# Softmax of the first four attention tiles on ScalarE, set by set, and an ordering-only dependency in the schedule planner

## The chip, the cores and the metric

One core of one Trainium2 chip. The metric is the device time in microseconds of one execution. Three runs of the kernel before lie between 1133.39 and 1134.48 us, with a median of 1134.45 us.

## The reference

Three stages run one after the other on 3072 tokens.

1. Chunked attention: batch 4, 8 heads, 768 positions, head size 64. Chunks of 32 queries see 8 memory keys and a window of 16 positions on the left, their own 32, and 8 on the right: 64 keys at most (fewer at the two ends of the sequence). Scores are `scale * q·k` with scale 1/8, then a softmax (`exp(s - max)`, divided by `sum + 1e-9`), then the product with the values.
2. A gated feed-forward layer: `(sigmoid(x @ w_gate) * (x @ w_val)) @ w_out`, with 512 features and 1536 hidden ones.
3. A second feed-forward layer with a rational function in place of the gate: `h = x @ w_in`, `P(h) / Q(|h|)`, `@ w_out`, with 2048 hidden features.

All in float32.

## The kernel before, in words

The 3072 tokens are 24 attention tiles of 128. A tile is 128 query rows by 8 sets (heads) of 64 keys, so its scores are 128x512. The weights come in as a packed form of 8 bytes an element: per unit of 128x512, two ScalarE operations (`conv_scale`: tile names `st` and `stp`) and one VectorE operation (`conv_bits`, into `wfgv` or `wfo`) make float32 of them. Each matmul operand is then split into a high part (ScalarE copy, `split_hi`) and a low part (VectorE subtraction, `split_lo`), both in the tile `wp`; three matmuls stand for one float32 product. A hidden block f of the first layer takes three units: 0 and 1 are the two halves of the contraction for gate and value together, 2 is the output weight.

The first four tiles (t = 0 to 3) make up the start of the kernel, together with the conversion of the weights of blocks 0, 1 and 2. TensorE's order there is written out by hand: scores (`sp`) of tile 0, 1, 2, 3, transposes (`tp`) of tiles 0 and 1, the value product (`xp`) of tile 0, transposes of tiles 2 and 3, value products of tiles 1, 2 and 3, with matmuls on a tile of ones (`idle`) in between, and then the first products of block 0 (`h`). PSUM has four banks for all of these (pool `ps`), given out in turn: `sp` takes two, `tp` one, `xp` two, a group of `h` one.

Softmax of one of these tiles before the change:

- `attn_max` (L584): VectorE takes the maximum over the keys (one pass over 512 columns where the scores have been copied to SBUF because of the mask, which is tile 0; else two passes over 256 in PSUM), then subtracts it (as many passes), into the SBUF tile `s`.
- `attn_exp`: one ScalarE activation of 128x512.
- `attn_sum`: VectorE sums 512 columns into 8 sums (`r`), adds 1e-9, takes the reciprocal. `attn_mul` multiplies.

Tiles 4 to 7 use the same functions later on, between the blocks of the first layer. Tiles 8 to 23 use other functions (`pair_max` and so on).

The order of work on each engine other than TensorE isn't written by hand. A class `Recorder` keeps each operation as a task with an estimated duration and a latest start (`late`), and `plan()` runs a list schedule over them: each engine takes, of the tasks that are ready in the model, the one with the earliest `late`. The instructions are emitted in that order. Loads (SyncE's DMA queue) are ordered in the same way. A tile's memory is a `Cell`; the first task that touches it is `c.first`, and every other task that touches the cell depends on it in `access` (L275), even where it works on other bytes of it. Two loads of different units into one tile are such a case: the weights of blocks 1 and 2 are loaded by `load_w1` into four tiles named `stp`, two units to a tile, so that units 0 and 1 of a block lie in the same tile.

Of the kernel before, what the change touches and what calls it, by code (L numbers as in the profile page):

```python
# [11 lines left out]
F32 = mybir.dt.float32  # L12
# [4 lines left out]
ACTF = mybir.ActivationFunctionType  # L17
ALU = mybir.AluOpType
AX = mybir.AxisListType
PSUM = bass.MemoryType.PSUM  # L20

B, H, S, D = 4, 8, 768, 64
CH, LEFT, RIGHT, NMEM = 32, 16, 8, 8
NT, DM, DFF1, DFF2 = B * S, H * D, 1536, 2048
P = 128
# [6 lines left out]
KEYS = NMEM + LEFT + CH + RIGHT  # L32
OFF1 = WIN - KEYS
NSET = 8
# [19 lines left out]
class Cell:  # L54


    def __init__(self, pool, make, dt, real=None):
        self.pool, self.make, self.dt, self.real = pool, make, dt, real
        self.accesses, self.users, self.first, self.group, self.left = [], set(), None, None, 0
# [115 lines left out]
class Task:  # L175
    def __init__(self, eng):
        self.eng, self.calls, self.deps, self.cells, self.gets = eng, [], set(), set(), []
        self.dur, self.lat, self.bytes, self.start, self.table, self.mark = 0.0, 0.15, 0, None, None, None
        self.window, self.cap, self.soon, self.late, self.fixed = 30.0, None, 0.0, 0.0, False
        self.ordered = True  # L180
# [10 lines left out]
class Recorder:  # L191
# [48 lines left out]
    def call(self, eng, op, args, kw):  # L240
        out = kw.get("out", args[0] if args else None)
        reads = [x for x in (*args[0 if "out" in kw else 1 :], *kw.values()) if isinstance(x, Ref) and x is not out]
        reads = [x for x in reads if x is not kw.get("out")]
        key = {x.cell for x in reads}
        if eng == "tensor" and out.size() > 128:
            key.add(out.cell)
        same = eng == "tensor" and self.open is not None and self.open.key == key
        if same:
            t = self.open
        else:  # L250
            t = Task(eng)
            t.key, t.fixed, t.soon = key, self.fixed, self.ideal
            self.tasks.append(t)
            if eng == "tensor":
                self.open = t
                t.late = t.soon = self.ideal
            if self.noted is not None:
                self.noted.append(t)
        before = t.dur
        self.cost(t, op, args, kw)  # L260
        if eng == "tensor":
            self.ideal += t.dur - before
        t.calls.append((op, args, kw))
        for x, write in [(x, False) for x in reads] + ([(out, True)] if isinstance(out, Ref) else []):
            self.access(t, x, write)
        if eng != "tensor" and self.open in t.deps:
            self.open = None

    def access(self, t, x, write):
        c, box = x.cell, x.box()  # L270
        if c.pool is not None and t not in c.users:
            if c.first is None:
                c.first = t
                t.gets.append(c)
            elif c.first is not t:  # L275
                t.deps.add(c.first)
            c.users.add(t)
            t.cells.add(c)
        keep = []
        for b, u, w in c.accesses:  # L280
            if b[0] < box[1] and box[0] < b[1] and b[2] < box[3] and box[2] < b[3]:
                if u is not t and (write or w):
                    t.deps.add(u)
                inside = box[0] <= b[0] and b[1] <= box[1] and box[2] <= b[2] and b[3] <= box[3]
                if write and inside or u is t and w == write and inside:
                    continue
            keep.append((b, u, w))
        keep.append((box, t, write))
        c.accesses = keep
# [24 lines left out]
    def plan(self):  # L314
        tasks = self.tasks
        for t in tasks:
            t.succ = []
        for t in tasks:
            t.missing, t.soft = len(t.deps), []
            for d in t.deps:  # L320
                d.succ.append(t)
            t.ready = 0.0
# [6 lines left out]
        for t in reversed(tasks):  # L329
            t.succ, t.hard = t.succ + t.soft, t.succ  # L330
            if t.eng == "tensor":
                t.late = min([t.soon] + [u.late - t.lat * (u.eng != "tensor") - t.dur for u in t.succ])
                continue
            lat = t.lat + (4.5 if t.bytes else 0)
            cap = t.cap if t.cap is not None else self.DMA_CAP if t.bytes else self.CAP
            t.late = min([t.soon + cap] + [u.late - lat - t.dur for u in t.succ])
        free = dict(self.sizes)
        cells = {c for t in tasks for c in t.cells}
        for c in cells:
# [14 lines left out]
        ready = {e: [t for t in tasks if t.eng == e and not t.missing] for e in engines}  # L354
        busy, dma, table = dict.fromkeys(engines, 0.0), 0.0, None
        order, ends, half, now, stall, left = [], [], None, 0.0, 0.0, len(tasks)
        events = []
        self.stalls = []
        while left:
# [3 lines left out]
            for e in engines:  # L363
# [10 lines left out]
                for t in pick:  # L374
# [7 lines left out]
                    need, h = {}, half  # L382
                    for c in t.gets:
                        if c.pool == ("t", "half"):
                            if h:
                                h = None
                                continue
                            h = True
# [8 lines left out]
                t = best  # L397
# [29 lines left out]
                for c in t.cells:  # L427
                    c.left -= 1
                    g = c.group
                    g[2] = max(g[2], end)  # L430
                    if c.left == 0:
                        g[1] += 1
                        if g[1] == 2 or g[1] == g[0] and g is not half:
                            heapq.heappush(ends, (g[2], self.real_pool(c.pool)))
                for u in t.hard:
                    u.missing -= 1
                    u.ready = max(u.ready, end if u.eng != e or e != "tensor" else now + t.dur)
                    if not u.missing and u.eng != "tensor":
                        ready[u.eng].append(u)
                    heapq.heappush(events, u.ready)  # L440
# [4 lines left out]
            if not moved:  # L445
# [5 lines left out]
                for e in engines[1:]:  # L451
                    for t in ready[e]:
                        w = t.late + stall - t.window
# [5 lines left out]
                now = max(nxt, now + 1e-6)  # L459
# [15 lines left out]
def fused_kernel(ctx: ExitStack, tc: tile.TileContext, q, k, v, w1, w2, coef, x2d, w2o, wq2, wqa, wqs, out):  # L475


    nc = Recorder(tc.nc)
    x2d, w2o, wq2, wqa, wqs = (cell_ref(None, None, x.shape, F32, x, True) for x in (x2d, w2o, wq2, wqa, wqs))

    def pool(name, bufs, **kw):
        return Pool(ctx.enter_context(tc.tile_pool(name=name, bufs=bufs, **kw)), name, bufs, nc.sizes)
# [6 lines left out]
    spool = pool("s", 4)  # L489
# [28 lines left out]
    qs, ks, vs, s_sb, sc_ps, at_sb = {}, {}, {}, {}, {}, {}  # L518
# [19 lines left out]
    def edge(t):  # L538
        return t % SB in (0, SB - 1)

    def attn_qk(t):
# [28 lines left out]
        else:  # L570
            sc_ps[t] = sps

    def attn_max(t):
        s = s_sb[t]
        m = spool.tile([P, NSET, 1], F32, tag="m", name=f"m{t}")
        if edge(t):
            nc.vector.tensor_reduce(out=m[:, :, 0], in_=s, axis=AX.X, op=ALU.max)
            nc.vector.tensor_tensor(out=s, in0=s, in1=m.to_broadcast([P, NSET, KEYS]), op=ALU.subtract)
            return
        sv = s.rearrange("p (r h) w -> p r h w", h=2)  # L580
        mv = m.rearrange("p (r h) w -> p r h w", h=2)
        sps = sc_ps.pop(t)
        for h in range(2):
            nc.vector.tensor_reduce(out=mv[:, :, h, 0], in_=sps[h], axis=AX.X, op=ALU.max)  # L584
        for h in range(2):
            nc.vector.tensor_tensor(
                out=sv[:, :, h], in0=sps[h], in1=mv[:, :, h].to_broadcast([P, 4, KEYS]), op=ALU.subtract
            )

    def attn_exp(t):  # L590
        s = s_sb[t]
        nc.scalar.activation(out=s, in_=s, func=ACTF.Exp, scale=1.0 / float(D) ** 0.5)

    rs = {}

    def attn_sum(t):
        s = s_sb[t]
        r = rs[t] = spool.tile([P, NSET, 1], F32, tag="r", name=f"r{t}")
        nc.vector.tensor_reduce(out=r[:, :, 0], in_=s, axis=AX.X, op=ALU.add)
        nc.vector.tensor_scalar_add(out=r, in0=r, scalar1=1e-9)  # L600
        nc.vector.reciprocal(out=r, in_=r)

# [582 lines left out]
    def at(si, *call):  # L1185
        plan.setdefault(si, []).append(call)
# [24 lines left out]
    for t in range(4, NPAIR, 2):  # L1211
        s0 = 2 if t == 4 else 5
        for o, u in ((0, t), (1, t + 1)):
            at(s0 + o - 2, load_qk, u)
            at(s0 + o, attn_qk, u)
            at(s0 + o, attn_max, u)
            at(s0 + 3, attn_exp, u)
            at(s0 + o + 3, load_v, u)
            at(s0 + o + 3, attn_sum, u)
            at(s0 + o + 3, attn_mul, u)  # L1220
            at(s0 + o + 4, attn_t, u)
            at(s0 + o + 5, pv, u)
# [89 lines left out]
    with tc.manual_schedule():  # L1312
# [14 lines left out]
        idle_mm(8)  # L1327
        attn_qk(0)
        attn_max(0)
        attn_exp(0)  # L1330
        idle_mm(2)
        attn_qk(1)
        idle_mm(3)
        attn_qk(2)
        attn_sum(0)
        attn_max(1)
        attn_exp(1)
        attn_max(2)
        attn_sum(1)
        idle_mm(12)  # L1340
        attn_qk(3)
# [724 lines left out]
```

## Time and profile before

| | us |
|---|---|
| median of 3 runs | 1134.45 |
| the profiled execution | 1134.46 |
| its span | 1132.6 |
| TensorE busy | 1120.2 (99%) |
| VectorE busy | 872.8 (77%) |
| ScalarE busy | 750.1 (66%) |
| GpSimd busy | 23.1 (2%) |

The span is what the instructions of the one profiled execution cover; its own time is 1.86 us longer. Busy shares are averages over stages that have different limits. The busy time of TensorE counts the matmuls on the tile of ones too.

### The profile page before, as it was taken

To read this page: it belongs to the slowest core of one execution; us is meant where nothing else is said; L and a number is where in the kernel's file an instruction comes from. 1 tells how busy PE (TensorE), PEld (TensorE's weight loads), DVE (VectorE), ACT (ScalarE), POOL (GpSimd) and SP (SyncE) were. 2 spreads that over 40 slices of the span, in tenths; PEclk is the share of its full clock that TensorE was granted. 3 is DMA by queue.
4 is the path that set the end of the run, shared out by engine and by line. 5 is a ranking of instruction groups with operands and counts; after the bars stand their busy time and mean duration, and the time that the engine had idled before them with its cause. 6 is when DMAs were issued, how large, how long until landed. Compare 5 with 4: busy or idle time off the path is not lost.

```text
span 1132.6 us, 20033 instructions
## 1 busy us (share of the span) xinstructions
PE 1120.2 (99%) x7815; PEld 918.5 (81%) x7815; DVE 872.8 (77%) x1184; ACT 750.1 (66%) x1105; POOL 23.1 (2%) x39
## 2 busy tenths in 40 slices
PE   8999999999999999999999999999999999999998
PEld 4787888888888888888888788888888888888887
DVE  5788867774676667565568499999899999789984
ACT  4999556663454466343345599875799974898852
POOL 0000000000000000000000000000000000000000
PEclk8999999999999999999999999999999999999999
DMA  9899699997978799898976576689677788576764
GB/s 371 311 352 360 227 347 363 350 365 259 379 279 324 288 376 387 310 373 291 322 259 246 191 230 220 208 246 342 203 229 225 223 288 307 167 242 219 230 207 143
DMA packets 100318, 318.78 MB, mean 281 GB/s; under 512 B 10752, under 2 KB 11008, under 8 KB 100224
## 3 DMA queue, kind: packets, MB, share of 16 engines
q1 hardware_dynamic: 96192, 303.51, 74.3%
q0 software_dynamic: 3456, 12.58, 6.0%
q8 instruction: 62, 1.02, 0.4%
q10 hardware_dynamic: 576, 1.41, 0.3%
q14 instruction: 32, 0.26, 0.1%
HBM read 240.91 MB, written 63.96 MB: 269 GB/s over the span
## 4 chain that ended last, share of the span: by engine, by line
PE 96%; ACT 1%; DMA 1%; DVE 1%; issue 0%; DVEq 0%
PE acc L471 40%; PE p L471 20%; PE q_X L471 12%; PE h L471 10%; PE q_Z L471 6%; PE q_Y L471 3%; PE xp L471 2%; PE sp L471 1%; PE tp L471 1%; PE idle L471 1%; DMA st<-w_in 0%; DMA k<-k_in 0%; ACT L471 0%; ACT stp L471 0%; DVE s L471 0%
## 5 line engine op out<-in xcount | busy, mean ns | idle before, releaser
L471 PE MATMUL acc<-w2o,G 128*128 128x512 f32 x1152 | 268.4, 389 | 0.0
L471 PEld LDWEIGHTS acc<-w2o,G 128*128 128x128 f32 x1152 | 216.2, 188 | 44.9
L471 PE MATMUL acc<-g,wp 128*128 128x512 f32 x720 | 177.0, 393 | 0.0
L471 PEld LDWEIGHTS acc<-g,wp 128*128 128x128 f32 x720 | 133.3, 188 | 28.3 <-issue 0.2
L471 PE MATMUL q_X<-x,wi 128*128 128x512 f32 x576 | 146.5, 390 | 1.4 <-ACT hb L471 1.4
L471 PE MATMUL h<-x,wp 128*128 128x512 f32 x576 | 138.1, 392 | 1.7 <-ACT sg L471 0.9
L471 PE MATMUL p<-b,wpq_s 128*128 128x512 f32 x576 | 138.4, 389 | 0.0
L471 PEld LDWEIGHTS q_X<-x,wi 128*128 128x128 f32 x576 | 107.9, 188 | 24.7 <-ACT hb L471 2.5
L471 PEld LDWEIGHTS h<-x,wp 128*128 128x128 f32 x576 | 107.2, 188 | 25.0 <-ACT wp L471 1.1
L471 PEld LDWEIGHTS p<-b,wpq_s 128*128 128x128 f32 x576 | 108.1, 188 | 22.5
L471 ACT ACTIVATE st<-st 128x512 f32<-128x512 f32 (+1 forms) x124 | 76.7, 666 | 0.0
L471 PE MATMUL p<-x,wpq_a 128*128 128x512 f32 x288 | 73.2, 389 | 0.0
L471 PE MATMUL q_Z<-x,wi 128*128 128x512 f32 x288 | 73.1, 389 | 0.0
L471 ACT ACTIVATE u<-q,qc 128x1024 f32<-128x1024 f32 x48 | 54.9, 1147 | 14.4 <-DMA q<-u 13.2
L471 PEld LDWEIGHTS p<-x,wpq_a 128*128 128x128 f32 x288 | 54.0, 188 | 11.3
L471 PEld LDWEIGHTS q_Z<-x,wi 128*128 128x128 f32 x288 | 54.1, 188 | 11.2
L471 DVE SCALAR_TENSOR_TENSOR t<-t,cf,u 128x1024 f32<-128x1024 f32 x48 | 61.2, 1278 | 0.0
L471 DVE SCALAR_TENSOR_TENSOR q<-q,u 128x1024 f32<-128x1024 f32 x48 | 58.3, 1219 | 2.2 <-ACT u L471 2.1
L471 ACT ACTIVATE hb<-q_X 128x512 f32<-128x512 f32 x48 | 28.4, 592 | 36.4 <-PE q_X L471 36.3
L471 ACT ACTIVATE u<-u 128x1024 f32<-128x1024 f32 x48 | 50.3, 1055 | 0.4
L471 ACT ACT_TABLE_LOAD x31 | 39.8, 1283 | 15.8 <-PE h L471 7.2
L471 ACT ACTIVATE g<-c 128x512 fp32r<-128x512 f32 x22 | 13.8, 629 | 51.1 <-DVE c L471 51.1
(271 smaller groups left out, 1708.8 us busy)
## 6 DMA issues: line engine op xcount, KB each, us to landing
w2o<-w2o SPq DMA_DIRECT2D x96, 512.0 KB, 4.4
wi<-wq SPq DMA_DIRECT2D x72, 512.0 KB, 4.6
st<-w_in SPq DMA_DIRECT2D x62, 512.0 KB, 7.0
wp<-wqa SPq DMA_DIRECT2D x55, 512.0 KB, 6.6
wpq_s<-wqs SPq DMA_DIRECT2D x48, 512.0 KB, 8.1
wpq_a<-wqa SPq DMA_DIRECT2D x36, 512.0 KB, 7.6
wqa<-wp SPq DMA_DIRECT2D x30, 512.0 KB, 7.5
v<-v_in SPq DMA_DIRECT2D x24, 512.0 KB, 6.4
```

Of the source, the lines that this page charges most:

```text
L471: getattr(getattr(self.nc, t.eng), op)(*[real(x) for x in args], **{n: real(x) for n, x in kw.items()})
```

## The change

For t < 4 the maximum is still taken by VectorE, but is no longer subtracted there. It is multiplied by -1/8 (a VectorE operation on 128x8, tile `nm`), and ScalarE takes the exponentials set by set: eight activations of 128x64 a tile in place of one of 128x512, each with its column of `nm` as the bias and with the sum of its row written beside (`accum_out`, into `r`). Three of the four tiles are read by ScalarE from PSUM. VectorE's subtraction and its sum are gone; the addition of 1e-9, the reciprocal and the multiplication stay. From tile 4 on all is as before.

In the recorder, a task that touches a cell after its first task now waits in the plan for the start of that first task only (`after`, `next`), not for its end. Dependencies on the data stay. `accum_out` counts as an output.

```diff
@@ access
                 c.first = t
                 t.gets.append(c)
             elif c.first is not t:
-                t.deps.add(c.first)
+                t.after.add(c.first)
@@ plan
-            t.missing, t.soft = len(t.deps), []
+            t.after -= t.deps
+            t.missing, t.soft = len(t.deps) + len(t.after), []
+            for d in t.after:
+                d.next.append(t)
@@ plan, latest starts (for tensor and for the rest)
-                t.late = min([t.soon] + [u.late - t.lat * (u.eng != "tensor") - t.dur for u in t.succ])
+                t.late = min([t.soon] + [u.late for u in t.next] + [u.late - t.lat * (u.eng != "tensor") - t.dur for u in t.succ])
@@ plan, when a task starts
+                for u in t.next:
+                    u.missing -= 1
+                    u.ready = max(u.ready, now)
@@ attn_max
-            nc.vector.tensor_tensor(out=s, in0=s, in1=m.to_broadcast([P, NSET, KEYS]), op=ALU.subtract)
...
+        if t < 4:
+            nm = nms[t] = spool.tile([P, NSET, 1], F32, tag="nm", name=f"nm{t}")
+            nc.vector.tensor_scalar(out=nm, in0=m, scalar1=-1.0 / float(D) ** 0.5, scalar2=None, op0=ALU.mult)
@@ attn_exp
+        nm = nms.pop(t)
+        r = rs[t] = spool.tile([P, NSET, 1], F32, tag="r", name=f"r{t}")
+        sps = sc_ps.pop(t, None)
+        for h in range(2):
+            for i in range(4):
+                a = 2 * i + h
+                nc.scalar.activation(
+                    out=s[:, a],
+                    in_=s[:, a] if sps is None else sps[h][:, i],
+                    func=ACTF.Exp,
+                    scale=1.0 / float(D) ** 0.5,
+                    bias=nm[:, a],
+                    accum_out=r[:, a],
+                )
@@ attn_sum
-        r = rs[t] = spool.tile([P, NSET, 1], F32, tag="r", name=f"r{t}")
-        nc.vector.tensor_reduce(out=r[:, :, 0], in_=s, axis=AX.X, op=ALU.add)
+        if t >= 4:
+            r = rs[t] = spool.tile([P, NSET, 1], F32, tag="r", name=f"r{t}")
+            nc.vector.tensor_reduce(out=r[:, :, 0], in_=s, axis=AX.X, op=ALU.add)
+        r = rs[t]
```

## Rows read from the trace of the kernel before

**Rows 1.** Chain of waits, 27 to 45 us: start, length, what.
```profile
35.30 1.28 ACT L471
37.83 0.69 DVE wp L471
38.57 3.92 PE h L471 x16
```
**Rows 2.** Waits, 44 to 117 us, then TensorE's from 117 us on: total, times, longest.
```profile
PE h L471 <- ACT sg L471: 0.9, 1, 0.9
...
PE q_X L471 <- ACT hb L471: 1.4, 2, 0.7
```
**Rows 3.** Windows: length, then busy (instructions) of five engines, granted clock, DMA.
```profile
15.00:20.80 5.80, 3.34 (x72) 2.83 (x72) 5.77 (x16) 4.00 (x7) 0.00 (x0) 0.72 1.03 405
20.80:24.20 3.40, 3.40 (x27) 2.16 (x19) 1.69 (x4) 2.74 (x7) 0.00 (x0) 0.50 1.04 404
...
38.60:117.00 78.40, 77.52 (x701) 62.88 (x702) 66.34 (x118) 77.90 (x137) 0.34 (x2) 1.00 0.94 346
```
**Rows 4.** Timeline, VectorE and ScalarE, 7 to 18 us: start, length, instruction, idle before.
```profile
7.50 0.69 DVE L471 TENSOR_REDUCE m<-s 128x8 f32<-128x512 f32 x1 [6.08 <-POOL s L471]
...
11.86 0.16 DVE L471 TENSOR_SCALAR r<-r 128x8 f32<-128x8 f32 x1
...
15.06 0.67 ACT L471 ACTIVATE stp<-stp 128x512 f32<-128x512 f32 x1 [1.46 <-DMA stp<-w_in]
...
17.14 0.63 ACT L471 ACTIVATE s<-s 128x512 f32<-128x512 f32 x1
```
**Rows 5.** Timeline, TensorE, 15 to 37 us.
```profile
15.92 0.63 PE L471 MATMUL tp<-ident,s 128*128 128x128 f32 x4 [1.59 <-DVE s L471]
...
19.11 1.93 PE L471 MATMUL xp<-at,v 64*64 64x32 f32 x64
20.97 1.97 PE L471 MATMUL tp<-ident,s 128*128 128x128 f32 x8
22.73 1.49 PE L471 MATMUL idle<-ones 128*128 128x512 bf16 x3
...
25.32 0.82 PE L471 MATMUL idle<-ones 128*128 128x512 bf16 x3
...
26.07 1.14 PE L471 MATMUL xp<-at,v 64*64 64x32 f32 x64
...
29.86 7.19 PE L471 MATMUL h<-x,wp 128*128 128x512 f32 x30
```
**Rows 6.** Groups of ScalarE instructions: durations (min/median/max ns, or busy us and mean ns).
```profile
L471 ACT ACTIVATE cab<-cf x2: 193/194/194, 576.6 to 583.2; 128x2 f32<-128x2 f32 x2
...
L471 ACT ACTIVATE u<-q,qc 128x1024 f32<-128x1024 f32 x48 | 54.9, 1147 | 14.4 <-DMA q<-u 13.2 <-DVE q L471 1.1
L471 ACT ACTIVATE u<-u 128x1024 f32<-128x1024 f32 x48 | 50.3, 1055 | 0.4
...
L471 ACT ACTIVATE s<-s 128x512 f32<-128x512 f32 x7 | 4.4, 631 | 4.5 <-DVE s L471 4.5
```
**Rows 7.** DMA issues by SyncE, 15 to 19 us; last the one at 17.61: KB, us to landing.
```profile
15.05 4.16 SPq L471 DMA_DIRECT2D stp<-w_in  x4
...
17.61 0.33 SPq L471 DMA_DIRECT2D stp<-w_in  x1
...
stp<-w_in SPq DMA_DIRECT2D x1, 512.0 KB, 9.1
```
**Rows 8.** Timeline, ScalarE and TensorE, 31 to 46 us.
```profile
31.78 3.50 ACT L471 ACTIVATE stp<-stp 128x512 int32<-128x512 uint32 x6
...
37.09 0.62 ACT L471 ACTIVATE wp<-wfgv 128x512 fp32r<-128x512 f32 x1
...
39.22 1.14 ACT L471 ACTIVATE wp<-wfgv 128x512 fp32r<-128x512 f32 x2
...
45.05 5.60 PE L471 MATMUL h<-x,wp 128*128 128x512 f32 x24
```

More of the change, by code (lines that the diff above doesn't have):

```diff
@@ L177, in __init__ @@
         self.eng, self.calls, self.deps, self.cells, self.gets = eng, [], set(), set(), []
+        self.after = set()
         self.dur, self.lat, self.bytes, self.start, self.table, self.mark = 0.0, 0.15, 0, None, None, None
@@ L242, in call @@
         reads = [x for x in (*args[0 if "out" in kw else 1 :], *kw.values()) if isinstance(x, Ref) and x is not out]
-        reads = [x for x in reads if x is not kw.get("out")]
+        reads = [x for x in reads if x is not kw.get("out") and x is not kw.get("accum_out")]
         key = {x.cell for x in reads}
@@ L263, in call @@
         t.calls.append((op, args, kw))
-        for x, write in [(x, False) for x in reads] + ([(out, True)] if isinstance(out, Ref) else []):
+        outs = [x for x in (out, kw.get("accum_out")) if isinstance(x, Ref)]
+        for x, write in [(x, False) for x in reads] + [(x, True) for x in outs]:
             self.access(t, x, write)
@@ L316, in plan @@
         for t in tasks:
-            t.succ = []
+            t.succ, t.next = [], []
         for t in tasks:
-            t.missing, t.soft = len(t.deps), []
+            t.after -= t.deps
+            t.missing, t.soft = len(t.deps) + len(t.after), []
+            for d in t.after:
+                d.next.append(t)
             for d in t.deps:
@@ L335, in plan @@
             cap = t.cap if t.cap is not None else self.DMA_CAP if t.bytes else self.CAP
-            t.late = min([t.soon + cap] + [u.late - lat - t.dur for u in t.succ])
+            t.late = min([t.soon + cap] + [u.late for u in t.next] + [u.late - lat - t.dur for u in t.succ])
         free = dict(self.sizes)
@@ L434, in plan @@
                             heapq.heappush(ends, (g[2], self.real_pool(c.pool)))
+                for u in t.next:
+                    u.missing -= 1
+                    u.ready = max(u.ready, now)
+                    if not u.missing and u.eng != "tensor":
+                        ready[u.eng].append(u)
                 for u in t.hard:
@@ L571, in attn_qk @@
             sc_ps[t] = sps
+    nms = {}
     def attn_max(t):
@@ L577, in attn_max @@
             nc.vector.tensor_reduce(out=m[:, :, 0], in_=s, axis=AX.X, op=ALU.max)
-            nc.vector.tensor_tensor(out=s, in0=s, in1=m.to_broadcast([P, NSET, KEYS]), op=ALU.subtract)
[L579 to L588, printed above, removed]
+            if t >= 4:
+                nc.vector.tensor_tensor(out=s, in0=s, in1=m.to_broadcast([P, NSET, KEYS]), op=ALU.subtract)
+        else:
+            sv = s.rearrange("p (r h) w -> p r h w", h=2)
+            mv = m.rearrange("p (r h) w -> p r h w", h=2)
+            sps = sc_ps[t] if t < 4 else sc_ps.pop(t)
+            for h in range(2):
+                nc.vector.tensor_reduce(out=mv[:, :, h, 0], in_=sps[h], axis=AX.X, op=ALU.max)
+            if t >= 4:
+                for h in range(2):
+                    nc.vector.tensor_tensor(
+                        out=sv[:, :, h], in0=sps[h], in1=mv[:, :, h].to_broadcast([P, 4, KEYS]), op=ALU.subtract
+                    )
@@ L590, in attn_exp @@
+        if t < 4:
+            nm = nms[t] = spool.tile([P, NSET, 1], F32, tag="nm", name=f"nm{t}")
+            nc.vector.tensor_scalar(out=nm, in0=m, scalar1=-1.0 / float(D) ** 0.5, scalar2=None, op0=ALU.mult)
+    rs = {}
     def attn_exp(t):
         s = s_sb[t]
-        nc.scalar.activation(out=s, in_=s, func=ACTF.Exp, scale=1.0 / float(D) ** 0.5)
-    rs = {}
+        if t >= 4:
+            nc.scalar.activation(out=s, in_=s, func=ACTF.Exp, scale=1.0 / float(D) ** 0.5)
+            return
+        nm = nms.pop(t)
+        r = rs[t] = spool.tile([P, NSET, 1], F32, tag="r", name=f"r{t}")
+        sps = sc_ps.pop(t, None)
+        for h in range(2):
+            for i in range(4):
[7 more added lines that the diff above has]
+                    accum_out=r[:, a],
+                )
@@ L596, in attn_sum @@
     def attn_sum(t):
         s = s_sb[t]
-        r = rs[t] = spool.tile([P, NSET, 1], F32, tag="r", name=f"r{t}")
-        nc.vector.tensor_reduce(out=r[:, :, 0], in_=s, axis=AX.X, op=ALU.add)
+        if t >= 4:
+            r = rs[t] = spool.tile([P, NSET, 1], F32, tag="r", name=f"r{t}")
+            nc.vector.tensor_reduce(out=r[:, :, 0], in_=s, axis=AX.X, op=ALU.add)
+        r = rs[t]
         nc.vector.tensor_scalar_add(out=r, in0=r, scalar1=1e-9)
```

## The prediction

> **What bounds the kernel now.** The page first: TensorE is busy 1120.2 of 1132.6 us, so only its idle or filler time can be won, and the slices show that in the first 40 us. Second the waits: past 44 us TensorE waits for other engines 0.9 us once and 1.4 us in two pieces [rows 2]. So the moment from which it runs without a break sets the end, one for one. Third the chain of waits around that moment: the products of block 1 go on at 38.57, released by the low part of its unit 1 (37.83, 0.69 long), which stands behind a high part on ScalarE at 37.09, which stands behind a table load of 1.28 and six conversions [rows 1, 8]. Fourth the windows ahead of it: from 15.0 to 20.8 VectorE is busy 5.77 of 5.80 us and TensorE's granted clock is 0.72, then 0.50 until 24.2 (mixtures of the levels 2.4 and 1.2 GHz), after it had waited for VectorE's softmax [rows 3, 5]. From 38.6 to 117 ScalarE is busy 77.90 of 78.40 us while TensorE hardly waits: ScalarE has little to spare there, which matters below.
>
> **The change part by part.**
>
> *VectorE.* Per tile a subtraction and a sum go, each about the 0.69 of the 512-column maximum [rows 4]; one operation on 128x8 comes, 0.16 [rows 4]. That is 1.2 us a tile, 4.9 us in all, most of it inside the stretch in which VectorE is full. Alone it would bring tile 3's softmax, and what follows, forward by about as much; ScalarE takes its place.
>
> *ScalarE.* Per tile one activation of 0.63 becomes eight of 64 columns. Such an instruction isn't in the trace. From 194 ns for 2 columns and 631 for 512 [rows 6] a line gives 247 ns at 64. A pointer operand costs 1147 - 1055 = 92 ns [rows 6] (other functions, same size), so 339. Neighbours overlap: six conversions take 3.50 where one takes 0.67 [rows 4, 8], that is (3.50 - 0.67) / 5 = 0.57 from start to start, 0.10 less than its duration. So 0.24 us each, if writing the sum beside costs nothing. If it costs one more smallest instruction (194 ns) that overlaps like the rest, 0.33; if nothing overlaps round it, 0.339 + 0.194 = 0.53. I take 0.33, the value that follows from rows if the sum is read out by an instruction like its neighbours, and keep 0.24 and 0.53 as ends. A tile is then 2.64 us (1.92 to 4.24) for 0.63.
>
> The Trainium skill, page "VectorE: DVE Perf Modes", section "Two Vector instructions with no wait between them", says that an operation that also writes out its accumulator is two instructions, the main one and a read of the accumulator. That is told of VectorE; no row here shows it of ScalarE. If it holds there, 0.24 drops out and the sum lies at the one given next or above it.
>
> *The path through the start.* Tile 0's maximum ends at 8.19; with the 0.16 and 0.1 for the hand-over, ScalarE starts at 8.45, and works through tiles 0, 1, 2 until 11.1, 13.75, 16.4, since it has nothing else then: the first weights land at 15.06 [rows 4]. Now PSUM: before, VectorE's subtraction freed the scores' banks, now the exponentials do. Scores 3 take tile 1's banks: 13.85 in place of 13.50, ready by 14.7, harmless. Transposes 0 and 1 take tile 2's, 15.1 and 16.5. One eviction (0.5), then tile 3's exponentials from 16.9 to 19.55; and the value product of tile 0 takes tile 3's two banks, so it starts at 19.65. Before it started at 19.11 [rows 5]: 0.55 later, though VectorE is far less loaded.
>
> From there to the first `h` it took 29.86 - 19.11 = 10.75. At full clock the value product, eight transposes and three fillers cost 1.14, 2 x 0.63 and 0.82 instead of 1.93, 1.97 and 1.49 [rows 5]: 2.2 less. Before that stretch TensorE waits about as much as now, so I expect a low clock again and give a third of it: 10.05, an estimate. First `h` at 29.7 (29.9 before). Thirty matmuls then run 6.8 us (7.19 with the pipeline's end [rows 5]), and at 36.5 block 1's second half is due. Before it had to wait until 38.57.
>
> *The order of loads and conversions.* Loads of units 0 and 1 of block 1 go into one tile. With `deps` the second was planned behind the landing of the first, and the first was pulled forward so that the second is in time. With `after` the second may follow at once. Of the four `stp` loads issued from 15.05, 1.28 apart, this second half is the third, at 17.61, and lands 9.1 later, at 26.7 [rows 7]. Sorted by its due time it stands behind the unit loads of block 0 and the values: in the slots of 1.28 from 15.05 on I count st, v, v, st, stp, stp, so about 21.5 (an estimate). The first `stp` load gives up its early slot to block 0's unit 0, which is wanted first. So the conversion of block 1's unit 1 no longer waits behind those of output weights and block 2 (five of the six in [rows 8] and one split, 3.4 us) nor behind the table load and a sigmoid (1.8): 5.2 us come off in front of the instruction at 37.09. Against that ScalarE has past 15.06 the tail of tile 2 (1.3) and 2.64 - 0.63 for tile 3, 3.3 more, with some 3 us of gaps between 15 and 25.5 (7 - 4.00 - 2.74 and what follows [rows 3]) to take it up, if work is ready there. So the high part falls between 32.2 and 35.2, the low part ends by 33.7 to 36.7: about in time for 36.5. Without the reordering the gain on TensorE's side would end in the same wait at 38.57.
>
> *Behind it.* The five conversions and the split moved back now compete with the next blocks'. Block 2's high parts came at 39.22 and were used at 45.05 [rows 8]: with the low parts some 3.5 us in hand, and ScalarE's total by 38.6 grows by 8.0 us (4 x 2.01) against about 7.7 us idle between 8.45 and 25.5. So it fits, narrowly.
>
> *Sum.* 36.5 - 38.57 = -2.1 us. The profiled execution took 1134.46, which is the median of the runs to 0.01: 1132.4. By the low end, 0.24: tile 3's maximum is ready at 15.35 and its exponentials at 17.3 (17.8 with an eviction), the first `h` at 26.4 to 28.6, block 1's second half 33.2 to 35.4: -3.2 to -5.4. By the high end, 0.53: tile 3 ends at 8.45 + 4 x 4.24 + 0.5 = 25.9, value product at 26.0, block 1's second half at 26.0 + 10.05 + 6.8 = 42.9: +4.3.
>
> **Rivals.**
>
> *A, cheap exponentials* (0.24): -3.2 to -5.4, of which ScalarE's narrow stretch behind takes one back; 1130.5. For it: the pointer's 92 ns and the overlap are measured. Against it: the sum must come out for nothing.
>
> *B, slower: ScalarE holds the PSUM banks.* The value product of tile 0 waits for the last exponential of tile 3. Break-even where 8.45 + 32c + 0.6 + 10.05 + 6.8 = 38.57, c = 0.40 us; at 0.53 it is +4.3, 1138.8; at 0.45, +1.7. For it: a read-out that lets nothing overlap. Against it: every ScalarE neighbour in the trace overlaps by 0.1.
>
> *C, given back.* TensorE starts 2 us earlier into a stretch in which ScalarE is 99% busy [rows 3], and the gain returns as waits such as the 0.9 for a sigmoid [rows 2]; the new order can also add a table load of 1.28 [rows 1]. Net nothing: 1134.4. For it: ScalarE's work grows by 8 us. Against it: 3.5 us in hand at block 2.
>
> *D, the order alone:* the changed ready times shuffle the plan further on and cost a wait of 1 to 3 us somewhere between 117 and 1132 us: 1135.5. Against it: few tiles there have two writers that don't depend by data.
>
> **How the numbers follow.** Forecast 40%, A 24%, B 15%, C 14%, D 7%. 0.2%, 2.3 us, is about what a measurement of this kernel can tell from no change: 1132.2 to 1136.7. Forecast's own range is 1131.0 to 1133.8; 16 of its 40 lie below 1132.2. Faster: 24 + 16 = 40. Same: 24 + 14 + 2 of B + 4 of D = 44. Slower: 13 of B + 3 of D = 16. The range 1129.3 to 1137.3 leaves out the far end of A (some 5) and of B (some 10).
>
> **What would show it.** In the timeline of the changed kernel: start-to-start of the 128x64 activations (0.33; above 0.40 B is on its way); whether they come with a second instruction; ScalarE without a gap from 8.45 to the end of tile 3 near 19.6; the value product of tile 0 right behind it (19.65); the clock from 20 to 25; the second `stp` load of block 1 ahead of the output weights; the second half of block 1 near 36.5 and not released by a ScalarE `wp`; TensorE's waits past 44 us still about 2.3 in all. If TensorE is in time at 36.5 and the kernel isn't faster, C or D; if the value product starts past 22, B. The forecast is wrong if the exponentials cost under 0.28 or over 0.40, or if the order past 45 us opens a new wait of over 1 us.

## The result, and the profile after

The changed kernel takes 1148.57 us (median; 1148.42 to 1148.85) where the kernel before takes 1134.05 (1133.39 to 1134.48) beside it: a ratio of 1.0127, 95% interval 1.0112 to 1.0142. That is 14.5 us slower; forecast were 1132.4, with a range of 1129.3 to 1137.3.

The page of the changed kernel: the span, each engine's busy time, and four of the costliest groups (busy us, mean ns of one | idle before).

```profile
span 1146.6 us, 20080 instructions
PE 1132.6 (99%) x7815; PEld 919.4 (80%) x7815; DVE 870.8 (76%) x1177; ACT 760.8 (66%) x1165; POOL 23.1 (2%) x39
...
L481 PE MATMUL acc<-w2o,G 128*128 128x512 f32 x1152 | 269.1, 390 | 0.0
...
L481 PE MATMUL q_X<-x,wi 128*128 128x512 f32 x576 | 149.9, 395 | 1.4 <-ACT hb L481 1.4
L481 PE MATMUL p<-b,wpq_s 128*128 128x512 f32 x576 | 141.8, 394 | 0.0
...
L481 PE MATMUL p<-x,wpq_a 128*128 128x512 f32 x288 | 73.5, 390 | 0.0
```

Two of these groups in the page of the kernel before:

```profile
L471 PE MATMUL q_X<-x,wi 128*128 128x512 f32 x576 | 146.5, 390 | 1.4 <-ACT hb L471 1.4
...
L471 PE MATMUL p<-b,wpq_s 128*128 128x512 f32 x576 | 138.4, 389 | 0.0
```

Of the 14.0 us between the two spans 12.4 are busy time of TensorE (1120.2 to 1132.6), so little of it is idle time. The same number of matmuls takes longer, and not all of them. Those that stream from tiles of pool `b` went up by five or six ns: `p<-b` from 389 to 394, `q_X` from 390 to 395, `q_Z` from 389 to 395 (the streamed tiles of `q_X`, `q_Y` and `q_Z` are named `x` in the page, but are the tiles `x2`, which lie in `b`). They are 1728 matmuls in all. `p<-x` and `acc<-w2o`, which stream from other pools, went up by one. (`h`, from 392 to 395, holds the stretch at a low clock that is shown further down.) The timeline shows the same: a row of 18 took 4.24 us before and takes 4.36 now, TensorE timeline of before and then of after:

```profile
502.37 4.24 PE L471 MATMUL p<-b,wpq_s 128*128 128x512 f32 x18
```

```profile
507.75 4.36 PE L481 MATMUL p<-b,wpq_s 128*128 128x512 f32 x18
```

The windows over 50 us of that stretch, before and after (length, then busy time and instructions of PE, PEld, DVE, ACT, POOL, then clock, DMA share, GB/s): the clock is 1.00 in both and no engine does more, yet 219 matmuls fit in place of 223.

```profile
500.00:550.00 50.00, 50.00 (x223) 41.38 (x222) 30.16 (x48) 19.34 (x33) 0.00 (x0) 1.00 0.88 308
```

```profile
500.00:550.00 50.00, 50.00 (x219) 40.68 (x217) 29.23 (x46) 18.89 (x32) 0.00 (x0) 1.00 0.88 303
```

Where the 14.0 us of the two spans arise is read from the chains of waits, before and after: the long stretch of `p` begins 1.67 later (256.12 to 257.79), and the rest, 12.3, comes behind it.

```profile
256.12 9.52 PE p L471 x42
```

```profile
257.79 9.72 PE p L481 x42
```

Now the rows that answer to those shown of before. ScalarE in the start [rows 4] and TensorE [rows 5], timeline of the changed kernel:

```profile
8.89 0.35 ACT L481 ACTIVATE s<-s,nm 128x64 f32<-128x64 f32 x1 [1.55 <-DVE nm L481]
9.14 0.19 ACT L481 ACTIVATION_READ_ACCUMULATOR s<-s,nm 128x1 f32 x1
...
9.42 0.31 ACT L481 ACTIVATE s<-sp,nm 128x64 f32<-128x64 f32 x1
...
9.72 0.31 ACT L481 ACTIVATE s<-sp,nm 128x64 f32<-128x64 f32 x1
...
18.70 1.20 ACT L481 ACTIVATE at<-tp 128x512 f32<-128x512 f32 x2
...
33.62 0.64 ACT L481 ACTIVATE wp<-wfgv 128x512 fp32r<-128x512 f32 x1
```

```profile
19.46 1.94 PE L481 MATMUL xp<-at,v 64*64 64x32 f32 x64 [2.12 <-ACT at L481]
21.32 1.97 PE L481 MATMUL tp<-ident,s 128*128 128x128 f32 x8
...
30.02 11.28 PE L481 MATMUL h<-x,wp 128*128 128x512 f32 x48
41.14 2.88 PE L481 MATMUL acc<-g,wp 128*128 128x512 f32 x12
```

The 48 matmuls in one row at 30.02 are blocks 0 and 1 without a break: the wait ahead of block 1's second half [rows 1, 8] is gone. The output products behind it begin at 41.14. In the kernel before the second half started at 37.76, and the output products here:

```profile
37.76 4.73 PE L471 MATMUL h<-x,wp 128*128 128x512 f32 x18 [0.71 <-ACT wp L471]
42.33 2.88 PE L471 MATMUL acc<-g,wp 128*128 128x512 f32 x12
```

So the start did gain, 1.2 us. The second load of block 1 follows the first at once, and lands 11.2 us after its issue [rows 7], near 21.8 (forecast about 21.5):

```profile
9.96 0.95 SPq L481 DMA_DIRECT2D stp<-w_in  x2
```

```profile
stp<-w_in SPq DMA_DIRECT2D x1, 512.0 KB, 11.2
```

The gain is lost again near 96 us. TensorE's waits of the changed kernel past 44 us [rows 2], its windows [rows 3], and the timeline of ScalarE and TensorE there:

```profile
PE h L481 <- ACT c L481: 2.1, 1, 2.1
PE q_X L481 <- ACT hb L481: 1.4, 2, 0.7
```

```profile
20.80:24.20 3.40, 3.40 (x35) 2.46 (x31) 0.76 (x2) 2.13 (x5) 0.00 (x0) 0.50 1.04 403
...
96.00:100.60 4.60, 4.57 (x13) 3.68 (x14) 2.05 (x4) 4.26 (x9) 0.00 (x0) 0.63 0.87 309
```

```profile
92.15 1.28 ACT L481 ACT_TABLE_LOAD   x1
93.44 0.63 ACT L481 ACTIVATE sg<-sg 128x512 f32<-128x512 f32 x1
94.09 1.28 ACT L481 ACT_TABLE_LOAD   x1
95.38 0.60 ACT L481 ACTIVATE c<-h 128x512 f32<-128x512 f32 x1
...
96.03 4.55 PE L481 MATMUL h<-x,wp 128*128 128x512 f32 x12 [2.13 <-ACT c L481]
100.42 1.76 PE L481 MATMUL acc<-g,wp 128*128 128x512 f32 x7
```

The same place before:

```profile
95.21 0.60 ACT L471 ACTIVATE sg<-h 128x512 f32<-128x512 f32 x1
...
95.86 3.02 PE L471 MATMUL h<-x,wp 128*128 128x512 f32 x12 [0.88 <-ACT sg L471]
98.72 2.88 PE L471 MATMUL acc<-g,wp 128*128 128x512 f32 x12
```

TensorE comes 1.1 us earlier, but the sigmoid, behind an exponential of a later tile between two table loads, ends at about the same time. The wait grows by 1.25 (0.88 to 2.13), and behind it the clock is 0.63 of full speed where it had stayed at 1.00, so the same 12 matmuls take 4.55 instead of 3.02: 1.53 more. Together 2.8, against the 1.1 by which TensorE came earlier: the output products start 1.7 later (98.72 to 100.42), as does `p`.

### The profile page after: what moved, and what is told of

The parts are those of the page before. It is cut to its first block, busy times and chain, and to the rows that moved or that the text cites. A ratio compares the mean times of both kernels' runs of the same rounds, so it can differ in the third digit from the quotient of the medians.

```text
span 1146.6 us, 20080 instructions
## 1 busy us (share of the span) xinstructions
PE 1132.6 (99%) x7815; PEld 919.4 (80%) x7815; DVE 870.8 (76%) x1177; ACT 760.8 (66%) x1165; POOL 23.1 (2%) x39
## 4 chain that ended last, share of the span: by engine, by line
PE 92%; ACT 6%; DMA 1%; DVE 1%; issue 0%; POOL 0%; ACTq 0%; DVEq 0%
PE acc L481 39%; PE p L481 20%; PE q_X L481 12%; PE h L481 8%; PE q_Z L481 6%; PE q_Y L481 3%; PE xp L481 2%; ACT st L481 2%; PE sp L481 1%; ACT s L481 1%; ACT wp L481 1%; PE tp L481 1%; ACT L481 1%; ACT stp L481 1%; DMA k<-k_in 0%; DMA wqa<-wp 0%
## 5 line engine op out<-in xcount | busy, mean ns | idle before, releaser
L481 PE MATMUL q_X<-x,wi 128*128 128x512 f32 x576 | 149.9, 395 | 1.4 <-ACT hb L481 1.4
L481 PE MATMUL p<-b,wpq_s 128*128 128x512 f32 x576 | 141.8, 394 | 0.0
L481 ACT ACTIVATE g<-c 128x512 fp32r<-128x512 f32 x23 | 14.5, 631 | 54.8 <-DVE c L481 54.8
```

Source lines behind the costliest of these rows:

```text
L481: getattr(getattr(self.nc, t.eng), op)(*[real(x) for x in args], **{n: real(x) for n, x in kw.items()})
```

## The experiments

Two causes had to be told apart and priced. T1: the four new `nm` tiles, 32 bytes a partition each, lie in pool `s`, which is laid out ahead of pool `b`; so every tile of `b` has moved up by 128 bytes against the weights, and matmuls that stream from there are slower. T2: the new order, which changes what runs beside them.

**1. `nm` behind `b`.** The changed kernel, with nothing moved but the place of the four tiles.

```diff
     bpool = pool("b", 8)
+    npool = pool("n", 4)
...
-            nm = nms[t] = spool.tile([P, NSET, 1], F32, tag="nm", name=f"nm{t}")
+            nm = nms[t] = npool.tile([P, NSET, 1], F32, tag="nm", name=f"nm{t}")
```

> The changed kernel, its order of work untouched, but the four small nm tiles (128 bytes a partition in all) lie behind the pool b instead of ahead of it, so that every other tile has the address that it had before the change. Theory T1 (addresses): in the changed kernel the matmuls that stream a tile of b take 233 ns start to start against 227 before, only because b lies 128 bytes higher; the address undone, they are back at 227, TensorE is busy some 12 us less and the time is 1136 to 1137: what is left is the 1.7 us by which it was late after the sigmoid at 96 us. Theory T2 (work): the new order of ScalarE, VectorE and loads slows the matmuls; then nothing changes, 1148.5, and p<-b stays at 233.

Measured: 1136.53 against 1134.77, ratio 1.0013 (1.0004 to 1.0021). Of its page and its TensorE timeline:

```profile
L481 PE MATMUL p<-b,wpq_s 128*128 128x512 f32 x576 | 138.3, 389 | 0.0
```

```profile
96.22 4.60 PE L481 MATMUL h<-x,wp 128*128 128x512 f32 x12 [2.13 <-ACT c L481]
```

The matmuls are as before and most of the loss is gone. The wait at 96 us is left; experiment 6 tests whether it accounts for the rest. Of the eleven executions eight had a mean granted clock of 0.995 and took 1135.83 to 1137.56, three had 0.997 and took 1134.30 to 1135.63. The trace is of one with 0.995, so the low clock behind the wait may not come every time; no second trace shows it.

**2. The kernel before, with pool `b` 128 bytes higher.** An unused tile, nothing else.

```diff
+    gap = pool("gap", 1).tile([P, 32], F32, name="gap")
     bpool = pool("b", 8)
```

> The kernel before with an unused 128 bytes a partition ahead of pool b; nothing else. T1: 1728 matmuls that stream from b take 233 instead of 227 ns, +11 to +12 us, 1145 to 1147, and the others stay. T2: 1134.5, since the order of the work is that of before.

Measured: 1146.59 against 1134.77, ratio 1.0105 (1.0092 to 1.0118). T1 holds: 11.8 us by the address alone, without any change of order. By the records of the two traces 10.5 of them lie in the 1728 matmuls that stream from `b`, which start 5.8 to 6.6 ns further apart. The others were not expected to change; their starts lie a little further apart too (`acc<-w2o` 0.6 ns, `p<-x` 1.3).

```profile
L471 PE MATMUL p<-b,wpq_s 128*128 128x512 f32 x576 | 141.8, 394 | 0.0
```

**3. The kernel before, everything 128 bytes higher.**

```diff
+    gap = pool("gap", 1).tile([P, 32], F32, name="gap")
     const = pool("const", 1)
```

> The kernel before with the same unused 128 bytes ahead of all pools, so that weights, streamed operands and all other tiles move up together. If the absolute address counts (T1a), every 128x512 matmul, some 4460, goes from 227 to 233 ns: +25 to +28 us, 1160 to 1163. If the distance between the streamed tile and others counts (T1b): no change, 1134.5. T2: 1134.5 as well.

Measured: 1134.50, ratio 0.9999 (0.9990 to 1.0007), the group again at 389 ns. It isn't the address itself but the distance between tiles.

**4. The order alone.** The recorder's part of the change on the attention of the kernel before.

```diff
-                t.deps.add(c.first)
+                t.after.add(c.first)
...
```

> The recorder's part of the change alone (a tile's place orders but no longer waits); softmax as before, addresses as before. By the prediction's step on loads and conversions the wait at 37 us for block 1 goes: second half of block 1 about 37.0 to 37.8 instead of 38.57, and the time 1133 to 1134.5, where the wait for the sigmoid near 95 us takes back what was won (theory C: ScalarE sets the time of that sigmoid, 0.9 becomes 1.7 or more and the time stays within 1 us of before). If the order itself costs something later on (D): above 1135.

Measured: 1138.24 against 1134.77, ratio 1.0038 (1.0024 to 1.0053), a miss. Block 1 no longer waits, but VectorE works in another order: the multiplication of the last tile stands behind the low part of tile 0's value product (`x<-xp,x`), which waits 1.44 us for ScalarE. It comes at 21.66; in the kernel before it came ahead of that low part, at 20.08. TensorE waits for it 0.59 us, and its granted clock from 24.20 to 31.00 is 0.83 (0.98 before). So the first `h` comes at 31.18 instead of 29.86, and nothing is won by 42 us (output products at 42.28). Then the wait at the sigmoid comes in this order too. VectorE of this kernel, the multiplication in the kernel before, and TensorE of this kernel:

```profile
21.32 0.42 DVE L481 TENSOR_TENSOR x<-xp,x 128x256 fp32r<-128x256 f32 x1 [1.44 <-ACT x L481]
21.66 0.68 DVE L481 TENSOR_TENSOR s<-s,r 128x512 f32<-128x512 f32 x1
```

```profile
20.08 0.68 DVE L471 TENSOR_TENSOR s<-s,r 128x512 f32<-128x512 f32 x1
```

```profile
22.49 1.09 PE L481 MATMUL tp<-ident,s 128*128 128x128 f32 x4 [0.59 <-DVE s L481]
...
31.18 11.27 PE L481 MATMUL h<-x,wp 128*128 128x512 f32 x48
...
96.93 4.41 PE L481 MATMUL h<-x,wp 128*128 128x512 f32 x12 [1.89 <-ACT sg L481]
```

**5. The exponentials alone,** `nm` behind `b` as in 1 and the second use of a tile planned behind the first one's landing, as before.

```diff
-                t.after.add(c.first)
+                t.deps.add(c.first)
```

> ScalarE's exponentials set by set alone, nm behind b so that no other address moves, and the recorder's dependencies as before. By the prediction's order step the loads of block 1 then come in the old order, its unit 1 stands behind conversions and the table load, and TensorE waits for it near 37 us: no gain there, 1134.5 to 1137. If the exponentials by themselves are a gain that the order spoils: below 1134.

Measured: 1138.55 against 1134.29, ratio 1.0039 (1.0026 to 1.0051), above what was expected.

```profile
39.91 5.86 PE L481 MATMUL h<-x,wp 128*128 128x512 f32 x18 [3.26 <-ACT wp L481]
45.60 2.88 PE L481 MATMUL acc<-g,wp 128*128 128x512 f32 x12
```

The second half of block 1 waits for its weights for 3.26 us. Behind the wait it starts slowly: the granted clock is 0.50 from 39.90 to 41.00, and 18 matmuls take 5.86 (4.73 before, with a further wait inside). The output products come at 45.60. In this planner the parts need each other: alone they cost 3.5 and 4.3 us, together (experiment 1) 1.8.

**6. Experiment 1, with the exponentials of later tiles kept near their due time.** The planner may place an instruction of ScalarE up to 30 us ahead of the time at which it is due; for exponentials past 20 us it is 12 now, so none with its two table loads lies ahead of that sigmoid.

```diff
+            if kw["func"] is ACTF.Exp and t.soon > 20:
+                t.window = 12
```

> The kernel of e1 (change, addresses undone), and the planner may take an exponential of tile 4 or later at most 12 us ahead of its due time, so that it no longer stands with its two table loads in front of a sigmoid. If the 2.1 us wait for that sigmoid near 96 us and the low clock behind it are what took the gain back (C): the wait goes, the stretch after it runs at full clock, and the time is 1131.5 to 1133.5. If ScalarE's total work is the limit there: the wait comes back at another place and the time stays at 1136.

**7. The kernel before with the same two lines.**

> The kernel before with the same rule for exponentials of tile 4 and later. It loses the 0.9 us wait for the sigmoid near 95 us: 1133.5 to 1134. Beside e6 it tells what the change itself is worth where the sigmoid doesn't take it back: by the start of block 1's output products (1.0 us earlier in the changed kernel) e6 should be 0.5 to 1.5 us faster than this one; if e6 isn't faster, the change is worth nothing at any address.

Measured: experiment 6 takes 1132.50 and experiment 7 1133.12, against 1134.29: ratios 0.9985 (0.9976 to 0.9993) and 0.9989 (0.9980 to 0.9998). Windows and timeline of experiment 6:

```profile
90.00:110.00 20.00, 20.00 (x209) 16.37 (x208) 16.49 (x33) 17.30 (x31) 0.00 (x0) 1.00 1.00 384
```

```profile
41.27 2.88 PE L483 MATMUL acc<-g,wp 128*128 128x512 f32 x12
```

No wait, clock 1.00, and the gain of the start is kept. The 1.8 us that experiment 1 loses thus belong to this wait. But the kernel before gains by the same rule, having waited 0.88 there, and somewhat more than expected. What the change itself is worth, without both mishaps, is 0.6 us (1132.50 to 1133.12), at the low end of what was expected. The start of the output products in experiment 7 says the same, 0.6 behind experiment 6:

```profile
41.89 2.88 PE L473 MATMUL acc<-g,wp 128*128 128x512 f32 x12
```

The two intervals overlap, as do the runs (1131.61 to 1133.37 and 1132.34 to 1133.82), so a gain of that size is likely, not shown.

**8 to 11. Distances,** one execution each: the unused tile of experiment 2 with 64, 256 and 32 bytes (8, 10 and 11), and one of 128 bytes (9) between the weights' pool and all that follow, so that every stream is displaced against its weights.

```diff
     wpool = pool("w", 20)
+    gap = pool("gap", 1).tile([P, 32], F32, name="gap")
     xpool = pool("x", 4)
```

> The kernel before with 64 unused bytes ahead of pool b. By T1b (the distance of the streamed tile to the weights decides) the matmuls streaming from b are slower than 227 ns here too if any distance that isn't a multiple of some larger step is bad: 1140 to 1147; if only 128 is bad: 1134.5.

> The kernel before with 128 unused bytes between pool w (which holds the split weights) and all the pools behind it: x, g, t and b move up together, w stays. If the distance between the streamed tile and the weight tile decides (T1b-w), the matmuls that stream from x and g are slow now as well as those from b: nearly all of some 4460 at 233 ns, 1158 to 1163. If it is the distance of b to x, g or t (tiles of the other streamed operands or of VectorE and ScalarE): as before, 1134.5, with 227 ns everywhere.

> The kernel before with 256 unused bytes ahead of pool b. If the slow distances repeat every 256 bytes: 227 ns for the matmuls from b and 1134.5. If every distance other than that of before is slow: 1143 to 1147.

> The kernel before with 32 unused bytes ahead of pool b. By a graded law (64 bytes cost 9.2 us, 128 cost 11.8): 4 to 9 us, 1138 to 1144. If only multiples of 64 bytes from the place of before are slow: 1134.5.

Measured, with the mean time from start to start of `p<-b`, worked out from the records of each trace (226.7 ns in the kernel before):

| displaced | bytes | us | against | start to start, ns |
|---|---|---|---|---|
| `b` | 32 | 1148.69 | 1134.62 | 233.5 |
| `b` | 64 | 1143.48 | 1134.29 | 230.0 |
| `b` | 128 | 1146.59 | 1134.77 | 232.6 |
| `b` | 256 | 1134.55 | 1134.62 | 226.7 |
| all but weights | 128 | 1160.12 | 1134.62 | 232.5 |

The page of the kernel with all streams displaced; here the groups that had stayed at 389 are slow too:

```profile
L471 PE MATMUL acc<-w2o,G 128*128 128x512 f32 x1152 | 275.9, 395 | 0.0
...
L471 PE MATMUL p<-b,wpq_s 128*128 128x512 f32 x576 | 141.7, 395 | 0.0
...
L471 PE MATMUL p<-x,wpq_a 128*128 128x512 f32 x288 | 74.7, 394 | 0.0
```

What counts is the distance of the streamed tile from pool `w`, and 256 bytes more cost nothing. Besides the weights that pool holds tiles on which VectorE and ScalarE work and into which loads land. The records of experiment 2 speak against these: the matmuls of `p<-b` start 232.6 ns apart on average where VectorE is busy for over nine tenths of the interval (254 of them) and 232.6 where it is busy for under a tenth (227); with ScalarE it is 232.7 (206) and 233.1 (303); where hardly any DMA packet is under way 232.7 (25). That leaves the weight tiles. That the cost grows with the distance was wrong: 32 bytes cost most, 64 least of those that cost. Weights moved by themselves, other distances and other types weren't tried, and why the chip does this stays open.

## Why the prediction was wrong

**The step that failed** is the one on VectorE: "one operation on 128x8 comes, 0.16". Its time was right, but it also writes a tile, four of 32 bytes, and their place wasn't looked at. That moved the tiles of `b`, and the 1728 matmuls that stream from there lost some 6 ns each: with what their neighbours lost, 11.8 us (experiment 2) of the 14.5. No rival held this, and the range had no term for it: without it the time is 1136.53 (experiment 1), inside the range.

**Two steps on what follows the start failed as well.** "So the moment from which it runs without a break sets the end, one for one": block 1's output products began 1.2 us earlier, and with the addresses undone the end came 1.8 later (experiment 1). "So it fits, narrowly": near 96 us it did not. ScalarE had an exponential with two table loads ahead of the sigmoid, and TensorE waited 2.13 us.

**Rival C was right in its place and wrong in its price.** Its "the gain returns as waits such as the 0.9 for a sigmoid" is what happened, at that very wait; "Net nothing" left out that the clock was low behind the longer wait (0.63, 1.53 us on 12 matmuls). Net it is +1.8 (experiment 1), which with 11.8 makes 13.6; the missing 0.9 lies within the intervals. The waits were priced as if TensorE, once late, were only late; rows of its waits must be read with the clock behind them.

**The forecast of the start held in its costs, less so in its path.** An exponential and its read-out took 0.29 us from start to start out of PSUM (the eight of tile 1, from 9.42 to 11.75) and 0.33 for tile 0 out of SBUF, against 0.33 taken; that there is a second instruction is shown by the row at 9.14. The Trainium skill, page "VectorE: DVE Perf Modes", section "Two Vector instructions with no wait between them", tells this of VectorE; by that rule the sum out of ScalarE is two instructions as well, and the trace agrees (0.19). So rivals A (0.24) and B (above 0.40) fall. ScalarE began at 8.89 (forecast 8.45). The value product started at 19.46 (19.65), but that the number fits is partly luck: it waited 2.12 us for ScalarE's copy `at`, which came behind tile 3's exponentials, at 18.70, where the forecast had one copy ahead of them and let the product wait for their banks. The first `h` came at 30.02 (29.7), the high part of block 1's unit 1 at 33.62 (32.2 to 35.2), and its second half had no wait.

The gain there was forecast at 2.1 us and was 1.2. Half of the difference is an error of the sum: it set 36.5, when the first of the second half's 18 matmuls is due, against 38.57, when the last 16 went on [rows 1]. The first two had run from 37.76, so two matmuls of 226.7 ns come off, and the sum should have read 1.6. The rest is mainly that the third of 2.2 us that a higher clock was to give back did not come (0.50 from 20.8 to 24.2, as before [rows 3]): from the value product to the first `h` it took 10.56, not 10.05. The "some 3 us of gaps" between 15 and 25.5 are right, though not the difference beside them: the two windows of [rows 3] are 9.2 us long together, not 7.

**"Without the reordering the gain on TensorE's side would end in the same wait"** was too mild: without it the wait became 3.26 us (experiment 5).

**Rival D,** "the order alone", was looked for past 117 us. It is real, but in the first 32 us and at the sigmoid, and costs 3.5 us when it comes without the exponentials (experiment 4).

## What to carry to other kernels

A change that adds a tile, however small, moves all that is laid out behind it: compare the addresses of tiles before and after, or put new small tiles last; when a profile shows one form of matmul slower by a few ns with the clock at 1.00, look there first. A wait of TensorE is not priced by its length alone: add what the matmuls behind it lose at a lower clock (here 1.53 us behind a wait of 2.13). When work is pulled forward, check what the planner puts in the time won on the engine that has least to spare, here ScalarE.

## What the runs showed of the hardware

- Matmuls of 128x512 ran at 226.7 ns from start to start with the streamed tile at its place of before or 256 bytes further from the weight tile in a partition, and at 230.0 to 233.5 with 32, 64 or 128 bytes more (experiments 2, 8, 10, 11). The Trainium skill, page "SBUF — State Buffer", section "Who interferes with whom", gives TensorE two independent read ports, one for the streamed operand and one for the weights; by that the distance would cost nothing. Experiments 2 and 9 differ from it (11.8 and 25.5 us), and the measurement decides.
- A wait of 2.13 us of TensorE was followed by a clock of 0.63 over the next 4.6 us, one of 0.88 at the same place by 1.00.
- An accumulator's read-out on ScalarE is an instruction of its own, 0.19 to 0.31 us long, that overlaps with its neighbours.
